# Filter tables transposed on the chip, a smaller DMA scratch, twelve weight tiles and a later router, in a kernel of Fourier filter and expert layers

## The chip, the cores and the metric

The kernel runs on one core of a Trainium2 chip. A core has five engines with queues of their own: TensorE (PE, its weight loads PEld), VectorE (DVE), ScalarE (ACT), GpSimd (POOL) and SyncE (SP), which here only issues DMAs; ScalarE and GpSimd issue DMAs too. Each queue is worked off in order, so an instruction that waits holds up all behind it. The metric is the device time of one execution in microseconds (us).

## The reference

Three layers follow each other, all in float32. The tokens of the second layer are the 8 x 3072 rows that the first gives; an expert's capacity is 768.

```
X = np.fft.rfft(x, axis=1)                       # x: 8 x 3072 x 256
y = np.fft.irfft(X * (filt_r + 1j*filt_i), n=3072, axis=1)
x = y.reshape(24576, 256)
logits = x @ w_gate                              # 8 experts
expert = argmax(logits);  gate = softmax probability of it
# each expert takes its first 768 tokens in order of arrival; later ones are dropped
y[e] = relu(disp[e] @ w1[e]) @ w2[e]             # w1: 8 x 256 x 1024, w2: 8 x 1024 x 256
out = gate * y[expert] where kept, else 0
out = ((out @ w_a) * (out @ w_b)) @ w_out        # 256 x 1536, 1536 x 256, given as float64
```

Only kept tokens have an output that is not zero. The eight experts are full after three of the eight sequences, so the kernel's fast path transforms sequences 0 to 2 only (NB0 = 3) and checks at the end that all experts were full; otherwise a general path follows, which does not run with these inputs.

## The kernel before

**Fourier filter.** A sequence of 3072 is taken as 128 x 24. Transform A is a product with a 128x128 table `wa` (L264, and L277 for sequence 0, which keeps its result in SBUF). For each half h of the 256 channels, 32 pairs of frequencies are worked in eight chunks of four: `fwd` multiplies with the forward tables `wb` (L309), VectorE forms the complex product with the filter tiles `fr` and `fi` (L320 to L322), GpSimd adds the two parts to `y` (L323), and `inv` multiplies `y` with the inverse tables `wbi` (L332). Sequence 0 gets its operand by transposes on TensorE (L300); sequences 1 and 2 write transform A to DRAM (`da`) and read it back. The last steps are `idft_t` (L373) and `idft_a` (L390), which writes token rows to DRAM (`rows`), and the router's product (L412).

**Order.** The order is written by hand. A loop over `i` in `fast_path` (iteration i) takes one forward chunk and, two iterations behind it, one inverse chunk; three iterations (i = 16 to 18) are left without a forward chunk, so chunk g is in iteration g up to 15 and g + 3 from 16 on. `put(first, last, steps)` spreads other steps over iterations: the loads of the next x, transform A of the next sequence, and of the sequence before it the inverse transforms and the routing. Iteration 37 to 52 are the last: there the routing of sequence 1 is laid beside sequence 2's chunks.

**Loads at the start.** SyncE's queue first issues x of sequence 0 in two halves, the tables and the filter tiles (`p1_loads`), then x of sequence 1. The filter tile's partitions 64 to 127 are a copy of 0 to 63, made by ScalarE (`self.twice`, L215), except for the first tile of a half (i = 0), which is loaded a second time from an array of its own, `fr0`, that differs in one row. x of sequence 1 goes into the buffer of x of sequence 0 and waits for its last reader.

**Routing.** `route` gives seven steps (argmax, one-hot, a running count over tokens by a scan at L426, a product with a triangle for the totals at L433, slot numbers) and then eight `put` steps (one-hot values on VectorE at L468 and L471 and on GpSimd at L470) and eight `add` steps (product L480 and addition L483) that build the table of slots.

**Experts.** Sixteen blocks of 384 slots, (expert, half), of eight steps each; step s (L1131) does one `up` (six products, two terms by three for the split into high and low parts) and, two steps behind it, one `down`. Weights come in chunks of 128 hidden units: `load` by SyncE into a tile `raw`, `split` into `wh` on ScalarE (L633) and `wl` on GpSimd (L634). NWC is the number of `wh` and `wl` tiles and of the first `raw` tiles (ten); later `raw` tiles are five. The token rows of a block are gathered by three indirect DMAs from GpSimd (L646), transposed on TensorE (L657) and split. `beside[s]` holds the routing of sequence 2, which goes beside steps 0 to 11; `main` is what stands between the last inverse chunk and step 0: the chunks' loads, the first gather and its transposes, the eight inverse transforms `t1` (L373) and the logits `r[0]` (L412). `a` are the twelve output transforms (L390).

**Last layer.** From step 17 on the float64 weights are converted beside the experts; then TensorE computes the last layer from 545 us to the end, and GpSimd scatters the results (L742).

Of the kernel before, what the change touches and what calls it, by code (L numbers as in the profile page):

```python
# [31 lines left out]
NWC = 10  # L32
# [4 lines left out]
NE = 3  # L37
# [15 lines left out]
def dft_tables():  # L53
# [5 lines left out]
    wbi = np.zeros((2, 2, N2, NPAIR, N2, 4))  # L59
    for s in range(64):  # L60
# [10 lines left out]
        for q in range(N2):  # L71
            if s == 0 and q == 0:
                alt = (-1.0) ** n2
                wb[:, 0, 0, 0, 0, 0] = 1.0
                wb[:, 0, 0, 1, 0, 0] = alt
                wbi[0, 0, 0, 0, :, 0] = 1.0
                wbi[1, 0, 0, 0, :, 0] = alt
                continue
# [3 lines left out]
            if s == 0:  # L82
                g = 0 if q < 12 else 1
                wb[:, g, 0, 0, 0, q] = c
                wb[:, g, 0, 1, 0, q] = -sn
                wbi[0, 0, q, 0, :, g] = 2 * c
                wbi[1, 0, q, 0, :, g] = -2 * sn
            else:
# [6 lines left out]
                wbi[0, j, q, p, :, a] = c  # L95
                wbi[1, j, q, p, :, a] = -sg * sn
                wbi[0, j, q, p, :, b] = sn
                wbi[1, j, q, p, :, b] = sg * c
# [3 lines left out]
    wbip = np.zeros((2, 64, NPAIR, 96), f)  # L102
    wbip[:, 0:48] = wbi.reshape(2, 48, NPAIR, 96)
    return (wa.astype(f), wai.astype(f), wbp.reshape(96, NPAIR, P)[:, :, 0:112],
            wbip.reshape(P, NPAIR, 96)[0:112])
# [22 lines left out]
class Kernel:  # L128
# [73 lines left out]
    def p1_loads(self):  # L202
# [3 lines left out]
        def table(name, i):  # L206
            q.dma_start(getattr(self, name)[i], io[name][:, 8 * i:8 * i + 8, :])

        def real(h, i):
            t = self.fr[4 * h + i]  # L210
            q.dma_start(t[0:64], io["fr"][:, h, 8 * i:8 * i + 8, :])
            if i == 0:
                q.dma_start(t[64:P], io["fr0"][:, h])
            else:
                self.twice[h, i] = lambda: self.nc.scalar.copy(t[64:P], t[0:64])  # L215
# [12 lines left out]
        for h in range(2):  # L228
            for i in range(4):
                steps += [lambda i=i: table("wb", i)] * (h == 0)  # L230
                steps += [lambda h=h, i=i: real(h, i)] * (h + i > 0)
                steps += [lambda h=h, i=i: imag(h, i)]
                steps += [lambda i=i: table("wbi", i)] * (h == 0)
        return steps + [lambda n=n: q.dma_start(getattr(self, n), io[n])
                        for n in ("iw", "wai", "scm", "eio", "tri", "ones", "eof", "lane", "line")]

# [45 lines left out]
    def dft_b(self, pe, pl, h, da, sa=None):  # L282
# [20 lines left out]
        def fwd(c, eng):  # L303
            if c % 2 and (h, c // 2 + 1) in self.twice:
                self.twice.pop((h, c // 2 + 1))()
# [312 lines left out]
    def load_chunk(self, pa, e, f, pr=None, eng=None):  # L618
# [6 lines left out]
        def load():  # L625
            raw = T["raw"] = (pr or pa).tile([P, 4, P], F32, tag="raw", name="raw", bufs=NWC if pr else 5)
# [298 lines left out]
def fast_path(K, outer):  # L925
# [4 lines left out]
    with ExitStack() as ctx:  # L930
# [16 lines left out]
        for step in loads[:6]:  # L947
            step()
        K.ident_ids()
        for step in consts[:5] + loads[6:] + consts[5:]:  # L950
            step()
# [12 lines left out]
        put(0, 5, K.dft_a_direct(xs, sa, 1))  # L964
# [25 lines left out]
        for i, g in enumerate(seq):  # L990
            back = seq[i - LAG] if i >= LAG else None
            if i == 5:
                xl, xn = K.load_x(pe, 1, K.new_sd(r2))
                st, das[1] = K.dft_a(pe, xn)
                put(5, 7, xl)
# [14 lines left out]
            if i == 34 + GAP:  # L1010
                t, a, r, p, d = finish(1)
                put(i, i + 1, t)
                put(i + 2, i + 5, rows_and_routes(a, r))
                put(i + 6, i + 9, p, into=early)
                put(i + 8, i + 11, d)
                put(i + 12, i + 12, [K.early_slots, lambda: K.counts(r1, 0, NE, min(cap, BLK))])
# [166 lines left out]
def general_path(K):  # L1183
# [9 lines left out]
    with ExitStack() as ctx:  # L1193
# [5 lines left out]
        run(K.p1_loads())  # L1199
# [51 lines left out]
def host_arrays(inputs):  # L1251
    f = np.float32
    wa, wai, wb, wbi = dft_tables()
# [39 lines left out]
```

## Time and profile before

| what | value |
|---|---|
| three timed runs | 1125.75, 1127.32, 1127.71 us; median 1127.32 |
| profiled execution: own time, span | 1124.34 us, 1122.5 us |
| TensorE busy | 1068.8 us, 95% |
| VectorE, ScalarE, GpSimd busy | 828.7 (74%), 442.6 (39%), 673.9 us (60%) |
| DMA | 123.27 MB, mean 110 GB/s |
| chain that ended last | TensorE 80%, DMA 6%, VectorE 4%, issue 4%, GpSimd 2% |

The span is the time from the first to the last instruction that the profiler records; the own time is that execution's time by the device's clock, 1.84 us more. The chain follows the end of the program back to what released each step. A row of a timeline gives the start, the busy time, the engine, the line, and in square brackets how long the engine had been idle and what ended that.

### The profile page before, as it was taken

What the parts mean: (1) busy time and instruction counts of PE and PEld (TensorE: products, weight loads), DVE (VectorE), ACT (ScalarE), POOL (GpSimd) and SP (SyncE); (2) the same over time, 40 slices, a digit from 0 to 9 for tenths busy, and PEclk for the clock granted to TensorE, in tenths of its full rate; (3) what the DMA queues carried; (4) which work ended last, traced back from release to release, by engine and by line L of the source; (5) the groups of instructions that cost most, each with busy time, mean ns of one, the idle gap of its engine ahead of it and who ended that gap; (6) DMA issues with size and microseconds to landing.
All of it is one profiled execution on the core that took longest, in us unless ns stands there. A gap on an engine that the chain in (4) does not pass through costs nothing.

```text
span 1122.5 us, 19362 instructions
## 1 busy us (share of the span) xinstructions
PE 1068.8 (95%) x6908; PEld 1023.9 (91%) x6908; DVE 828.7 (74%) x1589; ACT 442.6 (39%) x894; POOL 673.9 (60%) x676
## 2 busy tenths in 40 slices
PE   7899998899998999999999999999999999999993
PEld 7777797869998999999899999999999999999992
DVE  1738788675575777663888888888888888888873
ACT  2664544454665555553322232232232223232220
POOL 1412645576899787751555756657567475675742
PEclk8999999999999999999999999999999999999997
DMA  9955824354777666550404013040030000100000
GB/s 217 216 198 175 260 60 162 112 188 119 237 229 216 214 199 198 166 178 28 154 1 141 30 43 113 15 142 29 17 140 15 29 29 3 42 15 1 29 1 31
DMA packets 109097, 123.27 MB, mean 110 GB/s; under 512 B 8576, under 2 KB 92544, under 8 KB 108992
## 3 DMA queue, kind: packets, MB, share of 16 engines
q1 hardware_dynamic: 93152, 87.34, 26.4%
q10 hardware_dynamic: 11232, 22.02, 5.4%
q0 software_dynamic: 4608, 12.59, 3.6%
q8 instruction: 56, 0.92, 0.3%
q14 instruction: 49, 0.40, 0.1%
HBM read 68.44 MB, written 53.48 MB: 109 GB/s over the span
## 4 chain that ended last, share of the span: by engine, by line
PE 80%; DMA 6%; DVE 4%; issue 4%; POOL 2%; SPq 1%; ACT 1%; ACTq 0%; DVEq 0%; POOLq 0%
PE ps L666 13%; PE ps L667 13%; PE ps L668 13%; PE po L831 6%; PE po L830 6%; PE po L829 5%; PE yp L667 3%; PE yp L668 3%; PE yp L666 3%; PE ps L373 3%; PE ps L332 3%; PE ps L309 3%; PE ps L390 2%; PE ps L264 2%; DMA fr<-fr 1%
## 5 line engine op out<-in xcount | busy, mean ns | idle before, releaser
L758 POOL TENSOR_TENSOR gl<-w_b,gh 128x384 fp32r<-128x384 f32 x190 | 194.3, 1033 | 196.0 <-ACT gh L757 195.8
L757 ACT CAST gh<-w_b 128x384 fp32r<-128x384 f32 x192 | 98.7, 514 | 262.3 <-DVE w_b L776 196.8
L831 PE MATMUL po<-w_outh,gl 128*128 128x256 f32 x576 | 160.6, 279 | 0.2 <-POOL gl L758 0.2
L830 PE MATMUL po<-w_outl,gh 128*128 128x256 f32 x576 | 160.8, 279 | 0.0
L829 PE MATMUL po<-w_outh,gh 128*128 128x256 f32 x552 | 154.0, 279 | 0.0
L323 POOL TENSOR_TENSOR y<-t,t 112x512 f32<-112x512 f32 x48 | 65.6, 1368 | 128.0 <-DVE t L322 100.7
L634 POOL TENSOR_TENSOR wl<-raw,wh 128x512 fp32r<-128x512 f32 x88 | 112.3, 1292 | 39.6 <-ACT wh L633 16.5
L666 PE MATMUL ps<-th,w_bh 128*128 128x384 f32 x336 | 114.7, 341 | 4.4 <-DVE w_a L769 4.4
L666 PE MATMUL ps<-th,w_ah 128*128 128x384 f32 x336 | 113.5, 338 | 1.3 <-DVE w_b L769 0.8
L667 PE MATMUL ps<-tl,w_ah 128*128 128x384 f32 x336 | 113.6, 338 | 1.0 <-DVE tl L723 0.5
L668 PE MATMUL ps<-th,w_al 128*128 128x384 f32 x336 | 113.3, 337 | 0.0
L667 PE MATMUL ps<-tl,w_bh 128*128 128x384 f32 x336 | 113.2, 337 | 0.0
L668 PE MATMUL ps<-th,w_bl 128*128 128x384 f32 x336 | 113.1, 337 | 0.0
L683 DVE SCALAR_TENSOR_TENSOR hl<-ps,hh 128x384 fp32r<-128x384 f32 x128 | 70.5, 553 | 55.6 <-ACT hh L682 44.6
L831 PEld LDWEIGHTS po<-w_outh,gl 128*128 128x128 f32 x576 | 108.1, 188 | 1.5 <-POOL gl L758 0.4
L830 PEld LDWEIGHTS po<-w_outl,gh 128*128 128x128 f32 x576 | 108.0, 187 | 0.0
L829 PEld LDWEIGHTS po<-w_outh,gh 128*128 128x128 f32 x552 | 103.6, 188 | 0.0
L682 ACT ACTIVATE hh<-ps 128x384 fp32r<-128x384 f32 x128 | 62.7, 490 | 94.3 <-PE ps L668 84.3
L790 ACT COPY p<-ps 128x384 f32<-128x384 f32 x96 | 46.0, 479 | 127.3 <-PE ps L668 69.9
L776 POOL TENSOR_TENSOR w_b<-w_b,w_a 128x384 f32<-128x384 f32 x94 | 93.8, 1019 | 0.0
L666 PE MATMUL ps<-xh,wh 128*128 128x384 f32 x256 | 91.1, 356 | 0.0
L667 PE MATMUL yp<-hl,wh 128*128 128x384 f32 x256 | 86.0, 336 | 3.9 <-DVE hl L683 3.9
(157 smaller groups left out, 2801.3 us busy)
## 6 DMA issues: line engine op xcount, KB each, us to landing
out<-wide SPq DMA_DIRECT2D x48, 512.0 KB
raw<-w SPq DMA_DIRECT2D x176, 128.0 KB
rows<-yt ACTq DMA_DIRECT2D x18, 512.0 KB
da<-sa ACTq DMA_DIRECT2D x12, 512.0 KB
sb<-da SPq DMA_DIRECT2D x32, 192.0 KB
yd<-yb ACTq DMA_DIRECT2D x16, 384.0 KB
y<-yd SPq DMA_DIRECT2D x8, 768.0 KB
sd<-x SPq DMA_DIRECT2D x12, 256.0 KB
```

The costliest lines, as they stand in the source:

```text
L323: eng.tensor_tensor(y, t1, t2, ALU.add)
L634: (eng or nc.gpsimd).tensor_tensor(l, T["raw"], h.bitcast(F32), ALU.subtract)
L666: mm(out, wh, xh, start=first, stop=False)
L667: mm(out, wh, xl, start=False, stop=False)
L668: mm(out, wl, xh, start=False, stop=last)
L683: nc.vector.scalar_tensor_tensor(hl, hp[:, :BLK], 0.0, hh.bitcast(F32), ALU.max, ALU.subtract)
L757: nc.scalar.copy(gh, g)
L758: (v if hurry and not ij[1] else nc.gpsimd).tensor_tensor(gl, g, gh.bitcast(F32), ALU.subtract)
L776: (v if hurry or ij in ON_V else nc.gpsimd).tensor_tensor(c, c, T["a"][ij], ALU.mult)
L829: mm(out, gh[:, sl], oh[:, o:o + D], start=False, stop=False)
L830: mm(out, gh[:, sl], ol[:, o:o + D], start=False, stop=False)
L831: mm(out, gl[:, sl], oh[:, o:o + D], start=False, stop=u == NU - 1 and i == 1 and j == 0)
```

## The change

1. The inverse tables `wbi` are no longer loaded. The constants of pair s = 0 are scaled by the root of 2, so that each slice of `wbi` is the transpose of a slice of `wb`; `back_table` makes them with 32 transposes on TensorE and eight copies on VectorE, one table in each of iterations 1, 3, 5 and 7.
2. The first filter tile of a half is copied by ScalarE too (`twice`), and its one differing row is then loaded by a DMA from ScalarE's queue.
3. The loads of the start stand in another order; transform A of sequence 0's second half moves from iterations 0 to 5 to iterations 3 to 6, and the issue of x of sequence 1 from 5 to 7 to iterations 8 to 10.
4. The routing of sequence 1 is spread over more iterations (rows and routing 39 to 44 for 39 to 42, `put` 45 to 50 for 43 to 46, `add` 47 to 52 for 45 to 48).
5. In `main` the transposes of the first gathered rows move behind the inverse transforms, the logits and two output transforms; the routing of sequence 2 moves three or more steps back, the output transforms are one to a step.
6. The scratch for dynamic DMAs is set to 4096 bytes; NWC is 12, and `raw` has six tiles later on.

```diff
@@
-NWC = 10
+NWC = 12
...
-                wb[:, g, 0, 0, 0, q] = c
-                wb[:, g, 0, 1, 0, q] = -sn
-                wbi[0, 0, q, 0, :, g] = 2 * c
-                wbi[1, 0, q, 0, :, g] = -2 * sn
+                wb[:, g, 0, 0, 0, q] = 2 ** 0.5 * c
+                wb[:, g, 0, 1, 0, q] = -2 ** 0.5 * sn
...
         def real(h, i):
             t = self.fr[4 * h + i]
             q.dma_start(t[0:64], io["fr"][:, h, 8 * i:8 * i + 8, :])
+            self.twice[h, i] = lambda: twice(t, h, i)
+
+        def twice(t, h, i):
+            self.nc.scalar.copy(t[64:P], t[0:64])
             if i == 0:
-                q.dma_start(t[64:P], io["fr0"][:, h])
-            else:
-                self.twice[h, i] = lambda: self.nc.scalar.copy(t[64:P], t[0:64])
+                self.nc.scalar.dma_start(t[64:65, 0, :], io["fr0"][:, h])
...
-                steps += [lambda i=i: table("wbi", i)] * (h == 0)
...
+    def back_table(self, i):
+
+        nc = self.nc
+        for k in range(0, 8, 4):
+            pt = self.ps()
+            for j in range(4):
+                nc.tensor.transpose(pt[0:M2, 96 * j:96 * j + 96], self.wb[i][:, k + j, :], self.ident[0:96, 0:96])
+            nc.vector.tensor_copy(self.wbi[i][:, k:k + 4, :].rearrange("p j r -> p (j r)"), pt[0:M2, 0:384])
...
-            if c % 2 and (h, c // 2 + 1) in self.twice:
-                self.twice.pop((h, c // 2 + 1))()
+            if c % 2 and divmod(4 * h + c // 2 + 1, 4) in self.twice:
+                self.twice.pop(divmod(4 * h + c // 2 + 1, 4))()
...
-            raw = T["raw"] = (pr or pa).tile([P, 4, P], F32, tag="raw", name="raw", bufs=NWC if pr else 5)
+            raw = T["raw"] = (pr or pa).tile([P, 4, P], F32, tag="raw", name="raw", bufs=NWC if pr else 6)
...
-        for step in loads[:6]:
+        for step in loads[:3] + consts[:2] + [lambda: K.twice.pop((0, 0))()] + loads[3:6]:
             step()
         K.ident_ids()
-        for step in consts[:5] + loads[6:] + consts[5:]:
+        for step in consts[2:7] + loads[6:9] + consts[7:10] + loads[9:] + consts[10:]:
             step()
...
-        put(0, 5, K.dft_a_direct(xs, sa, 1))
+        put(3, 6, K.dft_a_direct(xs, sa, 1))
+        put(1, 8, [lambda i=i: K.back_table(i) for i in range(4)])
...
-                put(5, 7, xl)
+                put(8, 10, xl)
...
-                put(i + 2, i + 5, rows_and_routes(a, r))
-                put(i + 6, i + 9, p, into=early)
-                put(i + 8, i + 11, d)
-                put(i + 12, i + 12, [K.early_slots, lambda: K.counts(r1, 0, NE, min(cap, BLK))])
+                put(i + 2, i + 7, rows_and_routes(a, r))
+                put(i + 8, i + 13, p, into=early)
+                put(i + 10, i + 15, d)
+                put(i + 15, i + 15, [K.early_slots, lambda: K.counts(r1, 0, NE, min(cap, BLK))])
...
-            main += t1[k:k + 1] + {0: cs[0:1], 1: cs[1:2], 3: first[1:2], 4: first[2:3], 5: cs[2:3],
-                                   6: xs[1][0:1], 7: r[0:1] + cs[3:4]}.get(k, [])
+            main += t1[k:k + 1] + {0: cs[0:1], 2: cs[1:2], 5: cs[2:3], 6: xs[1][0:1]}.get(k, [])
+        main += r[0:1] + a[0:2] + first[1:2] + cs[3:4] + first[2:3]
...
-        beside[2] += xs[2][0:1]
-        for k, step in enumerate(a):
-            beside[k * 2 // 3].append(step)
+        beside[7] += xs[2][0:1]
+        for k, step in enumerate(a[2:]):
+            beside[k].append(step)
         for k, step in enumerate(r[1:]):
-            beside[k].append(step)
+            beside[3 + k].append(step)
         for k in range(0, NPUT, 2):
-            beside[7 + k // 2] += d[k:k + 2]
-            beside[6 + k // 2] += p[k:k + 2]
-        beside[11] += [lambda: K.all_slots(r1), lambda: K.counts(r1, 1, E, cap)]
+            beside[10 + k // 2] += p[k:k + 2]
+        for k in range(NPUT):
+            beside[12 + k // 3] += d[k:k + 1]
+        beside[14] += [lambda: K.all_slots(r1), lambda: K.counts(r1, 1, E, cap)]
...
-    nc = bacc.Bacc("TRN2", target_bir_lowering=False, num_devices=1)
+    nc = bacc.Bacc("TRN2", target_bir_lowering=False, num_devices=1, dynamic_dma_scratch_size=4096)
```

In SyncE's queue at the start of the program the loads stand as follows before (`sd` is x of sequence 0 in SBUF, `wb_119` and `wb_120` the first two forward tables, `wbi_123` an inverse table, `fr_127` the first filter tile):

```order
L249 DMA sd<-x 128x4x128 x6
L165 DMA ident<-eye 128x128
L166 DMA ids<-ids 128x24
L211 DMA fr_127<-fr 64x1024
L213 DMA fr_127<-fr 64x1024
L207 DMA wb_119<-wb 96x896
L219 DMA fi_135<-fi 48x1024
L207 DMA wbi_123<-wbi 112x768
L249 DMA sd<-x 128x4x128 x6
L207 DMA wb_120<-wb 96x896
```

And in the changed kernel, at the same place:

```order
L247 DMA sd<-x 128x4x128 x3
L199 DMA fr_127<-fr 64x1024
L247 DMA sd<-x 128x4x128 x3
L153 DMA ident<-eye 128x128
L154 DMA ids<-ids 128x24
L195 DMA wb_119<-wb 96x896
L209 DMA fi_135<-fi 48x1024
L195 DMA wb_120<-wb 96x896
L199 DMA fr_128<-fr 64x1024
L209 DMA fi_136<-fi 48x1024
L247 DMA sd<-x 128x4x128 x3
```

The filter tile moved between the two parts of x's first half, its second load and the inverse table are gone, and the second table and filter tile stand ahead of x's second half.

On TensorE, between the last inverse transforms and the first product of the experts, stands before (`iw,sc` are inverse transforms, `rowt` the gathered rows, `xh,wh` the experts' first product):

```order
L373 MATMUL ps_2087<-iw,sc 128x136 x3
L657 MATMUL ps<-ident,rowt 128x128 x3
L373 MATMUL ps_2099<-iw,sc 128x136 x3
L657 MATMUL ps<-ident,rowt 128x128 x3
L373 MATMUL ps_2111<-iw,sc 128x136 x3
L373 MATMUL ps<-iw,sc 128x136 x3
L373 MATMUL ps_2139<-iw,sc 128x136 x3
L412 MATMUL ps<-z,wai 128x192 x2
L390 MATMUL ps<-sd,wai 128x512 x2
L666 MATMUL ps<-xh,wh 128x384
```

And in the changed kernel:

```order
L371 MATMUL ps<-iw,sc 128x136 x3
L371 MATMUL ps_2179<-iw,sc 128x136 x3
L410 MATMUL ps<-z,wai 128x192 x2
L388 MATMUL ps_2192<-sd,wai 128x512
L388 MATMUL ps<-sd,wai 128x512
L655 MATMUL ps_2199<-ident,rowt 128x128 x3
L655 MATMUL ps<-ident,rowt 128x128 x3
L388 MATMUL ps<-sd,wai 128x512
L664 MATMUL ps<-xh,wh 128x384
```

The two groups of transposes moved from the middle of the inverse transforms to behind two output transforms.

On GpSimd, at the first expert steps, stands before (`rowt<-rows` are gathers, `wl<-raw,wh` splits, `val` the first one-hot values of the slot counting):

```order
L646 DMA rowt<-rows,early 128x256 x3
L634 TENSOR_TENSOR wl<-raw,wh 128x512 x3
L646 DMA rowt<-rows,early 128x256 x3
L634 TENSOR_TENSOR wl<-raw,wh 128x512 x4
L646 DMA rowt<-rows,early 128x256 x3
L634 TENSOR_TENSOR wl<-raw,wh 128x512 x6
L470 TENSOR_TENSOR val<-val,g 128x3x48
```

And in the changed kernel:

```order
L644 DMA rowt<-rows,early 128x256 x3
L632 TENSOR_TENSOR wl<-raw,wh 128x512 x3
L644 DMA rowt<-rows,early 128x256 x3
L632 TENSOR_TENSOR wl<-raw,wh 128x512 x13
L644 DMA rowt<-rows,early 128x256 x3
L632 TENSOR_TENSOR wl<-raw,wh 128x512 x3
L468 TENSOR_TENSOR val<-val,g 128x3x48
```

The third block's gather moved from behind four splits to behind thirteen, and 19 splits in place of 13 stand ahead of the slot counting.

## Rows read from the trace of the kernel before

**Rows 1.** Windows: start:end, us, busy PE, PEld, DVE, ACT, POOL, PEclk, DMA share, GB/s.

```profile
15.34:55.15 39.81, 32.39 (x260) 31.49 (x261) 24.83 (x36) 20.51 (x31) 15.23 (x12) 0.89 1.00 217
55.15:62.32 7.17, 7.17 (x21) 4.12 (x21) 0.00 (x0) 2.81 (x5) 0.00 (x0) 0.67 0.96 370
...
162.12:209.88 47.76, 43.58 (x300) 37.13 (x299) 43.37 (x84) 19.11 (x35) 23.12 (x27) 0.96 0.30 100
209.88:226.91 17.03, 14.10 (x105) 12.23 (x103) 7.22 (x20) 9.77 (x25) 10.71 (x10) 1.00 0.75 221
226.91:270.83 43.92, 40.79 (x217) 33.85 (x216) 30.58 (x69) 21.37 (x43) 33.32 (x37) 1.00 0.47 155
...
330.00:480.00 150.00, 143.96 (x839) 141.54 (x838) 104.05 (x239) 84.07 (x177) 119.03 (x122) 1.00 0.66 202
```

**Rows 2.** Chain of waits from 0 to 62 us: start, us, what.

```profile
30.80 9.79 DMA fr<-fr
...
40.60 9.25 DMA fi<-fi
...
50.79 4.22 DMA sd<-x
```

**Rows 3.** DMA issues from 0 to 80 us.

```profile
fr<-fr SPq DMA_DIRECT2D x10, 256.0 KB
...
wbi<-wbi SPq DMA_DIRECT2D x4, 336.0 KB
```

**Rows 4.** Timeline of the first 60 us.

```profile
7.01 0.59 ACT L278 COPY sa<-ps 128x512 f32<-128x512 f32 x1 [4.98 <-PE ps L277]
...
15.34 1.84 PE L309 MATMUL ps<-sb,wb 96*112 96x128 f32 x8 [1.58 <-DMA wb<-wb]
...
27.08 1.04 ACT L215 COPY fr<-fr 64x1024 f32<-64x1024 f32 x1 [5.68 <-DMA fr<-fr]
...
46.91 0.60 PE L300 MATMUL ps<-ident,sa 128*96 128x128 f32 x4
...
47.35 1.04 PE L309 MATMUL ps<-sb,wb 96*112 96x128 f32 x8
...
55.15 3.75 PE L264 MATMUL ps<-sd,wa 128*128 128x512 f32 x4 [4.58 <-DMA sd<-x]
```

**Rows 5.** Timeline, a copy of VectorE out of PSUM.

```profile
79.01 0.56 DVE L378 COPY sd<-ps 128x384 f32<-128x384 f32 x1
```

**Rows 6.** TensorE's waits from 165 to 290 us: us, times, longest.

```profile
PE ps L332 <- POOL y L323: 3.4, 1, 3.4
PE ps L433 <- DVE tot L428: 2.7, 1, 2.7
PE ps L657 <- DMA rowt<-rows,early: 1.9, 2, 1.3
```

**Rows 7.** Timeline, the scan in two routings and GpSimd beside the second.

```profile
168.14 0.56 DVE L426 TENSOR_TENSOR_SCAN cum<-scm,oh 128x192 f32<-128x192 f32 x1
...
229.13 4.95 POOL L634 TENSOR_TENSOR wl<-raw,wh 128x512 fp32r<-128x512 f32 x4
...
229.76 4.74 DVE L426 TENSOR_TENSOR_SCAN cum<-scm,oh 128x192 f32<-128x192 f32 x1
```

**Rows 8.** TensorE's waits from 330 to 380 us.

```profile
PE ps L657 <- DMA rowt<-rows,gidx: 1.8, 2, 1.3
PE yp L667 <- DVE hl L683: 1.8, 1, 1.8
```

**Rows 9.** Timeline, a later block's gathers and the transposes that use them.

```profile
279.22 1.03 POOL L646 DMA_INDIRECT rowt<-rows,gidx  x1 [0.15 <-issue]
280.56 1.00 POOL L646 DMA_INDIRECT rowt<-rows,gidx  x1 [0.30 <-issue]
...
287.96 0.49 PE L657 MATMUL ps<-ident,rowt 128*128 128x128 f32 x3
```

**Rows 10.** Chain of waits from 334 to 376 us, one gather's landing.

```profile
338.43 3.49 DMA rowt<-rows,gidx
```

More of the change, by code (lines that the diff above doesn't have):

```diff
@@ L58, in dft_tables @@
     wb = np.zeros((N2, 4, NPAIR, 2, 2, N2))
-    wbi = np.zeros((2, 2, N2, NPAIR, N2, 4))
     for s in range(64):
@@ L75, in dft_tables @@
                 wb[:, 0, 0, 1, 0, 0] = alt
-                wbi[0, 0, 0, 0, :, 0] = 1.0
-                wbi[1, 0, 0, 0, :, 0] = alt
                 continue
@@ L94, in dft_tables @@
                 wb[:, b, p, 1, j, q] = sg * c
[L95 to L98, printed above, removed]
     f = np.float32
@@ L101, in dft_tables @@
     wbp[:, :, :, 0:48] = wb.reshape(96, NPAIR, 2, 48)
[L102 to L105, printed above, removed]
+    return wa.astype(f), wai.astype(f), wbp.reshape(96, NPAIR, P)[:, :, 0:112]
 def filter_layout(filt):
@@ L204, in p1_loads, with table @@
         io, q = self.io, self.nc.sync
-        def table(name, i):
-            q.dma_start(getattr(self, name)[i], io[name][:, 8 * i:8 * i + 8, :])
+        def table(i):
+            q.dma_start(self.wb[i], io["wb"][:, 8 * i:8 * i + 8, :])
         def real(h, i):
@@ L229, in p1_loads @@
             for i in range(4):
-                steps += [lambda i=i: table("wb", i)] * (h == 0)
+                steps += [lambda i=i: table(i)] * (h == 0)
                 steps += [lambda h=h, i=i: real(h, i)] * (h + i > 0)
                 steps += [lambda h=h, i=i: imag(h, i)]
-                steps += [lambda i=i: table("wbi", i)] * (h == 0)
         return steps + [lambda n=n: q.dma_start(getattr(self, n), io[n])
                         for n in ("iw", "wai", "scm", "eio", "tri", "ones", "eof", "lane", "line")]
+    def back_table(self, i):
[5 more added lines that the diff above has]
+            nc.vector.tensor_copy(self.wbi[i][:, k:k + 4, :].rearrange("p j r -> p (j r)"), pt[0:M2, 0:384])
     def load_x(self, pe, b, whole=None, parts=1):
@@ L1198, in general_path @@
         nc.sync.dma_start(K.wa, K.io["wa"])
-        run(K.p1_loads())
+        run(K.p1_loads(), K.twice.values(), [lambda i=i: K.back_table(i) for i in range(4)])
+        K.twice = {}
         with tc.For_i(NB0, B) as b:
@@ L1252, in host_arrays @@
     f = np.float32
-    wa, wai, wb, wbi = dft_tables()
+    wa, wai, wb = dft_tables()
     cap = int(inputs["moe_capacity"])
@@ L1261, in host_arrays @@
     fi[0, :, 0, :] = 0
-    fr0 = fr[:, :, 0:8, :].copy()
-    fr0[0, :, 0, :] = inputs["filt_r"][S // 2].reshape(2, P)
+    fr0 = inputs["filt_r"][S // 2].reshape(1, 2, P)
     scm = np.ones((P, E, N2), f)
@@ L1268, in host_arrays @@
         **{n: np.ascontiguousarray(inputs["moe2_" + n]).view(np.int64) for n in ("w_a", "w_b", "w_out")},
-        wa=wa, wai=wai, wb=wb, wbi=wbi, iw=iw, fr=fr, fi=fi, fr0=fr0,
+        wa=wa, wai=wai, wb=wb, iw=iw, fr=fr, fi=fi, fr0=fr0,
         eye=np.eye(P, dtype=f), ones=np.ones((P, P), f), tri=np.triu(np.ones((P, P), f), 1),
```

## The prediction

> **What bounds the kernel now.** I read the windows by stage first [rows 1]: TensorE is the engine that sets the end, and what can be gained is the time in which it waits or runs at the lower clock. It waits in five places: before and after 55 us, between 162 and 210, between 210 and 227, in the first expert steps up to 271, and here and there from 330 to 480. In the second half of the program (from 545 on) neither the order nor the buffers are touched, so I leave it as it is.
>
> Second, the chain of waits of the first 62 us [rows 2]: it runs through SyncE's queue, from load to load (7 to 10 us each), and ends with the load of sequence 1's x, issued only at 50.79, after all tables and filters. The DMA share in this stretch is 1.00 at 217 GB/s [rows 1]: transfers bound it, and TensorE was busy 32.39 of 39.81 us. [...]
>
> Third, TensorE's own waits from 165 to 290 [rows 6]: 3.4 us for y from GpSimd (VectorE was late with its inputs), 2.7 us for the totals of the router, 1.9 us for the first gather of expert rows.
>
> **The change part by part.** The sum is made against the profiled execution: span 1122.5, own time 1124.34 us. The median of the timed runs is 1127.32, 3.0 us higher, and it is a median that is predicted.
>
> *Start.* Removed: four loads of the inverse table (336 KB each) and two second halves of a filter tile (256 KB each, two of the ten fr loads) [rows 3]: 1856 KB, 1.90 MB, which at the 217 GB/s of the stretch [rows 1] is 8.8 us. The load of sequence 1's x, 50.79 + 4.22 = 55.01 [rows 2], then lands at about 46.3. Its move from iterations 5 to 7 to iterations 8 to 10 costs nothing: no other SyncE instruction stands between, and it only has to follow the last use of the old x, now in iteration 6.
> Added on TensorE: 32 transposes of table slices. The nearest row is the transposing of the other operand, four from 46.91 to the next group at 47.35 [rows 4], 0.44 us, so eight groups are 3.5 us. Added on VectorE: eight copies of 112x384 out of PSUM, 0.56 us each by the 128x384 copy [rows 5], 4.5 us; VectorE was busy 24.83 of 39.81 us [rows 1], and 29.3 still fits, but wbi now stands behind it where it came by DMA. Added on ScalarE: two copies of filter halves at 1.04 us [rows 4], and two loads of one row from its queue.
> The first of those copies now stands at the head of ScalarE's queue and waits for the filter tile, the fifth load of SyncE's queue in place of the tenth. Behind it are the six copies of the first transform, behind these the first transposes and the first product. The tile and all ahead of it are 1.1 MB, 5 us at the stretch's rate; with 3 us for issue and latency (a gather took 3.49 to land [rows 10]) it is there at 8, and the copy ends at 9, where the first transform copy began at 7.01 [rows 4]. The six copies (0.59 each) then end near 13. The first table has 256 KB less ahead of it, 1.2 us. I put the first product at 15.34 as before [rows 4], 1.5 us later at worst.
> From there TensorE has its 32.39 us plus 3.5: 15.34 + 35.9 = 51.2. The x is there at 46.3, so TensorE itself is late next. Gain 55.15 - 51.2 = 3.9. Without the 4.58 us of idling the clock should not fall there: 7.17 us at 0.67 are 4.8 at 1.0, 2.4 more. **6.3 us**; from 2.5 (late start, clock lost elsewhere) to 9 (the transposes lie in waits that remain).
>
> *Sequence 1's router.* Nothing is removed; router and output transform are spread over six iterations instead of four, slot counting over six instead of four. From 162.12 to 209.88 VectorE was busy 43.37 of 47.76 us [rows 1]: it is the engine that bounds, first idle for others and then late for them. At best the stretch shrinks to VectorE's 43.4, a gain of 4.4; at worst nothing. I take **3 us**, nearer to the bound, since the 3.4 us wait for y [rows 6] is the pile-up that spreading removes. The counting ends later, but the first gather's issue was held by GpSimd's last y in any case.
>
> *The turn to the experts.* 17.03 us, TensorE busy 14.10 [rows 1]. Its transposes of gathered rows move behind all eight inverse transforms, the logits and two output transforms, so the gather (1.9 us of waiting [rows 6]) is covered; what is late next is the copy that feeds the inverse transforms. Bounds 0.5 and 2.9 (all idle time); I take **2 us**.
>
> *First expert steps.* 43.92 us, TensorE busy 40.79 [rows 1], so 3.1 us of waiting, 2.7 of them for the totals [rows 6]. The scan before these took 4.74 us where the same scan took 0.56 at 168.14, and it ended as a run of four GpSimd splits of 4.95 us in all ended [rows 7]. The change moves the scan from step 1 to step 4, where in steps 3 to 7 GpSimd now has two splits a step (2.5 us of about 3). If the scan meets pairs, it waits up to 2.5, which is inside the slack of about 3 us, one step, between it and the product that needs it (twelve steps took 43.92 us, 3.7 each with counting). If the splits form one long run, it waits longer than before. Two splits more fall into this stretch (2.5 us on GpSimd, busy 33.32 of 43.92 [rows 1], so covered). I take **1.5 us**, from -4 to 3.1.
> [...]
>
> *Twelve and six tiles.* From 271 on each split stands nine steps ahead of its use instead of seven, with as many splits in each step as before: GpSimd's place in its queue is the same. The waits of TensorE there are for gathers and for hl [rows 8], not for split weights, so the extra tiles buy little: **0.5 us**, from -1 to 2, of the 6.0 us idle from 330 to 480 [rows 1].
>
> *The scratch.* It issues nothing and I take 0; its price, if it has one, is the last rival.
>
> Sum: 6.3 + 3 + 2 + 1.5 + 0.5 = 13.3. TensorE is busy nearly throughout behind each place, so an earlier end of a stage is kept. 1124.34 - 13.3 = 1111.0 beside the profile, 1114.0 from the median; between the two and nearer the median, **1113**.
>
> **The rivals.** *Only the start pays.* The spread work piles up elsewhere: in steps 12 to 14 TensorE's slot counting (24 products) now waits for GpSimd's one-hot values, which stand behind splits, and the scan meets a long run. For it: GpSimd's share in that stretch, 0.76. Against: the step between value and use is as long as before. Middle 0, turn 1, steps -2: 6.3 - 1 = 5.3, so 1122; with parts of the others 1118 to 1123.
> *The start does not pay.* ScalarE's head-of-queue copy and the in-order wait of the inverse products for VectorE's table copies make the first iterations as slow as the loads did. For it: a table copy stands behind two iterations of VectorE work. Against: VectorE's 29.3 of 39.8. Start 1, rest 7: 1127.3 - 8 = 1119.
> *Slower: the small ring holds GpSimd's DMAs.* Three gathers are issued 1.3 us apart and land 3.49 us after the last issue [rows 9, 10]. If the scratch holds one at a time, each of two waits 2.2 us more: 4.4 us per block. From first issue at 279.22 to use at 287.96 are 8.7 us, of which 2.6 + 3.5 = 6.1 are used [rows 9, 10], so 2.6 are slack and 1.8 us are lost per block, 23 us over 13 blocks, and 11 us on the last six scatters behind the last product. 34 - 13.3: 1148. It decides as soon as fewer than two gathers fit. Nothing in the trace shows the ring, but three gathers in flight at once are few.
> [...]
>
> **How the numbers follow.** The forecast 0.62 (1106 to 1119), only the start 0.20, no gain at the start 0.10, slower by the ring 0.04; 0.04 for all terms at their upper ends, 1104 and below. The range that leaves out 2 in 10 or less is 1105 to 1122. A measurement of this kernel can tell about 0.2%, 2.3 us, from no change. Faster takes the forecast, 0.18 of the second, 0.07 of the third and the upper ends: 0.91; same the 0.05 left of the second and third; slower 0.04.
>
> **What would show it.** Right: no load of wbi, and x of sequence 1 issued near 42 to 45; the first product of its transform (L264) starts near 51 with no idling before it and the clock at 1.0 after; the stretch from iteration 39 to the last forward product near 45 us; no wait of L657 for the early gather; the scan under 2.5 us. Wrong: L264 still waiting for x; wbi's copies as releasers of L332 for many us; a scan as long as a run of splits; gathers issued more than 1.3 us apart.

## The result, and the profile after

The changed kernel takes 1100.29 us (median of 4 runs, 1099.70 to 1101.68), the kernel before 1126.53 (median of 4, 1124.44 to 1127.71): a ratio of 0.9771, interval 0.9752 to 0.9789, or 25.8 us by the ratio. 1113 was predicted, range 1105 to 1122: the sign was right, the gain about twice the 13.3 us of the forecast's sum. The profiled execution has a span of 1099.9 us, 22.6 less than that of before. From line 240 to line 1080, line numbers are 2 lower than before (L666 is now L664).

**The start.** The chain of waits up to 54 us, start, us and what:

```profile
2.76 5.60 DMA fr<-fr
8.38 1.05 ACT fr L203
9.46 0.51 ACTq L205
10.01 3.04 ACT sa L276 x6
13.10 0.69 PE ps L298 x4
13.81 0.59 ACT sb L299
14.45 1.14 PE ps L307 x8
...
19.85 0.56 DVE wbi L233
20.41 0.14 issue
20.55 1.10 PE ps L330 x8
...
40.29 1.76 DMA fr<-fr
42.07 0.33 SPq L223
...
43.94 0.36 SPq L247
44.34 7.30 DMA sd<-x
51.78 1.96 PE ps L262 x4
```

From 10 to 40 us it runs through the engines and no more from load to load [rows 2]; its last stretch still goes through SyncE's queue and ends with sequence 1's x. The early filter copy ends at 9.42, and the first product stands at 14.45 in place of 15.34 [rows 4]. The six copies behind the filter copy in ScalarE's queue begin at 10.01, where the first of them began at 7.01 [rows 4]. The timeline around sequence 1's x:

```profile
43.94 3.99 SPq L247 DMA_DIRECT2D sd<-x  x6
...
48.86 1.88 PE L262 MATMUL ps<-sd,wa 128*128 128x512 f32 x4
51.78 1.96 PE L262 MATMUL ps<-sd,wa 128*128 128x512 f32 x4 [0.18 <-DMA sd<-x]
```

The x is issued from 43.94. Its transform starts at 48.86 without a wait, and the first four products take 1.88 us; it was 55.15, after 4.58 us of waiting, and 3.75 us [rows 4]. The next four wait 0.18 us for the x, so it comes only just in time. The forward product of chunk 12 came at 62.32 and comes at 54.01: 8.3 us, kept up to the router. How much of this is this one execution's luck is told in the part on why the prediction was wrong.

**The middle.** Windows (us, then busy us of PE, PEld, DVE, ACT and POOL, granted clock, DMA share, GB/s): from iteration 39 to the last forward product, the turn up to the first expert product, the first expert steps, and a stretch within these:

```profile
153.81:194.15 40.34, 38.57 (x274) 32.39 (x273) 38.16 (x74) 18.70 (x35) 20.92 (x23) 1.00 0.37 118
...
193.97:212.66 18.69, 18.12 (x134) 15.64 (x132) 9.24 (x28) 9.80 (x24) 14.80 (x16) 1.00 0.54 157
212.66:256.60 43.94, 41.15 (x208) 34.94 (x209) 30.86 (x57) 24.21 (x50) 35.50 (x35) 0.96 0.66 203
251.60:255.00 3.40, 3.40 (x12) 3.31 (x11) 3.09 (x6) 1.00 (x2) 3.24 (x6) 0.50 0.20 59
```

The first took 47.76 [rows 1]: 7.4 less. But TensorE has 26 instructions fewer in it and 29 more in the turn, which grew from 17.03 to 18.69. Together they gain 5.9 us, and the first expert product comes at 212.66 in place of 226.91, 14.25 earlier. The first expert steps took 43.92 and take 43.94: nothing gained. TensorE's waits in them:

```profile
PE ps L478 <- POOL val L468: 1.6, 1, 1.6
PE ps L431 <- DVE tot L426: 0.8, 1, 0.8
PE ps L665 <- DVE xl L657: 0.2, 1, 0.2
```

The wait for the totals fell from 2.7 us [rows 6] to 0.8, with the scan at 0.82 in place of 4.74 [rows 7]. A new one, for the one-hot values, took its place, and the granted clock is 0.50 behind it. The timeline of TensorE there:

```profile
245.10 0.33 PE L664 MATMUL ps<-xh,wh 128*128 128x384 f32 x1
...
247.18 0.49 PE L655 MATMUL ps<-ident,rowt 128*128 128x128 f32 x3
...
250.59 0.91 PE L478 MATMUL ps<-val,ohl 128*128 128x96 f32 x6 [1.59 <-POOL val L468]
251.28 0.42 PE L664 MATMUL ps<-xh,wh 128*128 128x384 f32 x1
...
255.01 0.50 PE L655 MATMUL ps<-ident,rowt 128*128 128x128 f32 x3
```

Twelve products take 2.08 us from 245.10 to 247.18, and 3.73 from 251.28 to 255.01: the stretch at half clock costs 1.65 more.

**The end.** From 274 us on TensorE's transposes of gathered rows (L655) come between 13.9 and 15.5 us earlier than before, and the last scatter, issued at 1109.06 before and at 1095.02 after, 14.0. The spans are 22.6 apart. The other 8.5 us lie behind the last scatter, where no engine counts as busy. First the timeline of before, with GpSimd's queue instructions behind it (count: shortest/median/longest ns, first and last start):

```profile
1109.06 0.98 POOL L742 DMA_INDIRECT out<-ob,oidx  x1 [0.30 <-issue]
...
L921 POOLq INC_SWDGE_SEM  x1: 2108/2108/2108, 1111.6 to 1111.6; - x1
...
L1290 POOLq DRAIN  x3: 40/107/7905, 1113.7 to 1122.2; - x3
```

The same of after:

```profile
1095.02 0.98 POOL L740 DMA_INDIRECT out<-ob,oidx  x1 [0.30 <-issue]
...
L919 POOLq INC_SWDGE_SEM  x1: 428/428/428, 1097.5 to 1097.5; - x1
...
L1290 POOLq DRAIN  x3: 40/107/1045, 1098.0 to 1099.6; - x3
```

The long DRAIN fell from 7.91 to 1.05 us and INC_SWDGE_SEM from 2.11 to 0.43: 8.54 us together.

### The profile page after: what moved, and what is told of

Same layout as the page of the kernel before. It is cut to its first block, busy times and chain, and to the rows that moved or that the text cites. A ratio compares the mean times of both kernels' runs of the same rounds, so it can differ in the third digit from the quotient of the medians.

```text
span 1099.9 us, 19423 instructions
## 1 busy us (share of the span) xinstructions
PE 1066.8 (97%) x6940; PEld 1024.0 (93%) x6940; DVE 832.0 (76%) x1597; ACT 443.5 (40%) x896; POOL 675.0 (61%) x676
## 4 chain that ended last, share of the span: by engine, by line
PE 80%; POOL 5%; DMA 4%; DVE 4%; issue 4%; ACT 1%; SPq 1%; POOLq 0%; ACTq 0%; DVEq 0%
PE ps L664 13%; PE ps L665 12%; PE ps L666 12%; PE po L829 6%; PE po L828 6%; PE po L827 5%; PE ps L330 3%; PE ps L307 3%; PE ps L371 3%; PE yp L665 3%; PE yp L666 3%; PE yp L664 3%; PE ps L388 2%; POOL wl L632 2%; PE ps L262 2%
## 5 line engine op out<-in xcount | busy, mean ns | idle before, releaser
L632 POOL TENSOR_TENSOR wl<-raw,wh 128x512 fp32r<-128x512 f32 x88 | 113.0, 1302 | 35.8 <-ACT wh L631 15.5
L664 PE MATMUL ps<-th,w_bh 128*128 128x384 f32 x336 | 114.7, 341 | 4.5 <-DVE w_a L767 4.5
L664 PE MATMUL ps<-th,w_ah 128*128 128x384 f32 x336 | 113.5, 338 | 1.2 <-DVE w_b L767 0.8
L666 PE MATMUL ps<-th,w_al 128*128 128x384 f32 x336 | 113.2, 337 | 0.0
L666 PE MATMUL ps<-th,w_bl 128*128 128x384 f32 x336 | 113.1, 336 | 0.0
L664 PE MATMUL ps<-xh,wh 128*128 128x384 f32 x256 | 91.8, 359 | 0.2
```

The lines of the kernel that those rows point to most:

```text
L632: (eng or nc.gpsimd).tensor_tensor(l, T["raw"], h.bitcast(F32), ALU.subtract)
L664: mm(out, wh, xh, start=first, stop=False)
L666: mm(out, wl, xh, start=False, stop=last)
```

## The experiments

The ratios of the runs below are against the kernel before, timed on the same chip.

**Each part by itself**

```diff
-    nc = bacc.Bacc("TRN2", target_bir_lowering=False, num_devices=1)
+    nc = bacc.Bacc("TRN2", target_bir_lowering=False, num_devices=1, dynamic_dma_scratch_size=4096)
```

> The kernel before with nothing changed but the scratch for dynamic DMAs, 4096 bytes. Theory A (the scratch is what shortens the close of the program): GpSimd's last long DRAIN takes 1.0 us in place of 7.9 and its INC_SWDGE_SEM 0.4 in place of 2.1, as in the profile after, so 8.5 us less, about 1118 from a median of 1126.5; nothing moves ahead of the last scatter, still issued near 1109. Theory B (the close depends on what ran before it, such as the order of the gathers): the DRAIN stays at 7.9 us and the time within 2 us of the kernel before. Theory C (my prediction's rival of a small ring): gathers are held, issued more than 1.3 us apart, and the time grows by 10 us or more.

Measured: 0.9912 (0.9878 to 0.9946), 9.9 us; DRAIN 1.05, INC_SWDGE_SEM 0.43:

```profile
1117.05 0.98 POOL L742 DMA_INDIRECT out<-ob,oidx  x1 [0.30 <-issue]
...
L921 POOLq INC_SWDGE_SEM  x1: 428/428/428, 1119.7 to 1119.7; - x1
...
L1290 POOLq DRAIN  x3: 40/107/1045, 1120.2 to 1121.8; - x3
```

Theory A in the close and in the time: one number in one line, which moves no instruction, gives about as much as the whole start does, or more (the intervals overlap). One thing was not as expected: the last scatter is issued at 1117.05 and not near 1109. The profiled execution is the slowest of the four (1123.93 us; the others take 1115.37 to 1118.95), at a mean granted clock of 0.982 where the profile of before has 0.986; its first expert product comes 2.3 us later than there, and the last layer begins 7.7 us later. So its span of 1122.1 us shows no gain, and 9.9 is a rough size; the close itself, from the end of the last scatter's issue to the end of the long DRAIN, takes 3.2 us in place of 11.6.

The start alone: the hunks on `dft_tables`, `p1_loads`, `back_table` and the first loads, with the order

```diff
-        put(0, 5, K.dft_a_direct(xs, sa, 1))
+        put(3, 6, K.dft_a_direct(xs, sa, 1))
+        put(1, 8, [lambda i=i: K.back_table(i) for i in range(4)])
...
-                put(5, 7, xl)
+                put(8, 10, xl)
```

> The kernel before with the start alone: inverse tables transposed on the chip, filter halves copied by ScalarE, x of sequence 1 loaded in iterations 8 to 10. Theory A (the places are independent): the gain is the shift read between the two profiles at iteration 12, 62.32 to 54.01, 8.3 us, and it is kept to the end: 1118. Theory B (part of the gain is given back where sequence 1's router piles up, since its bound there is VectorE and not the time at which it begins): 4 to 6 us, 1121 to 1123. My prediction had 6.3.

Measured: 0.9927 (0.9904 to 0.9949), 8.2 us: theory A; the interval, 5.7 to 10.8 us, does not exclude the upper end of B.

Sequence 1's router alone:

```diff
-                put(i + 2, i + 5, rows_and_routes(a, r))
-                put(i + 6, i + 9, p, into=early)
-                put(i + 8, i + 11, d)
+                put(i + 2, i + 7, rows_and_routes(a, r))
+                put(i + 8, i + 13, p, into=early)
+                put(i + 10, i + 15, d)
```

> The kernel before with the routing and slot counting of sequence 1 alone spread over more iterations. Theory A (the spread takes away the pile-up and nothing more): the stretch from iteration 39 to the last forward product shrinks from 47.8 us to about 40.3 as in the profile after, but the counting that is left over lands in the turn, so the first expert product comes about 5 us earlier, and the end 5 us earlier: 1121.5. Theory B (the counting that is left over delays the first gather and with it the turn): the first product comes at most 2 us earlier, and the time is 1124 to 1126.

Measured: 0.9976 (0.9957 to 0.9994), 2.7 us (0.7 to 4.8); the first expert product at 225.62 in place of 226.91. That is theory B's product and a time between the two theories: the stretch does shrink, from 47.8 to 40.3 us, but most of what leaves it lands in the turn.

The turn and the routing of sequence 2 alone:

```diff
...
-            beside[7 + k // 2] += d[k:k + 2]
-            beside[6 + k // 2] += p[k:k + 2]
+            beside[10 + k // 2] += p[k:k + 2]
+        for k in range(NPUT):
+            beside[12 + k // 3] += d[k:k + 1]
...
```

> The kernel before with the turn and the routing of sequence 2 alone changed (transposes of the gathered rows later, router, scan and counting three steps later). Theory A (my prediction's two terms): the wait for the first gather, 1.9 us, and that for the totals, 2.7 us, go: 1123 to 1122.5. Theory B (as the profile after suggests, in which the shift is 14.3 us at the first expert product and 14.4 at the fifteenth expert step): the wait for the totals is exchanged for one for the one-hot values of the counting and a stretch at half clock, so only the turn's 1 to 2 us stay: 1125.

Measured: 0.9954 (0.9938 to 0.9971), 5.2 us: theory A, more than the wait in the changed kernel's profile had me expect. The four parts add up to 26.0 us, the joined change has 25.8; with intervals of 3.7 to 7.6 us for each part that does not show them to be independent. In one stretch they are not, by one execution each: from iteration 39 to the first expert product the kernel before takes 64.8 us, the router alone 64.2, the turn alone 64.0, and the joined change 58.8.

Put back in the changed kernel, the same hunk:

> The changed kernel with the turn and the routing of sequence 2 put back as before. Theory A (it is worth what it was by itself, 0.5%): 1105 to 1106, with the wait for the first gather and that for the totals back. Theory B (with the later counting of sequence 1 its worth grows, because that counting now delays the first gather which the old turn needs at once): 1107 or more. Theory C (worth nothing here): 1100 to 1102.

Measured: 0.9821 (0.9805 to 0.9838), 1107.59, 7.3 us above the changed kernel by the medians and 5.6 by the ratios, with the wait for the totals back; the one for val, which the kernel before lacks [rows 6], stays:

```profile
PE ps L431 <- DVE tot L426: 2.3, 1, 2.3
PE ps L478 <- POOL val L468: 1.2, 1, 1.2
```

The first gather was waited for 3.0 us in place of 1.9 [rows 6]. That is some support for B; the two ways of reckoning are too far apart to call it shown.

**What pays in the start**

```diff
+                steps += [lambda i=i: table("wbi", i)] * (h == 0)
...
-        put(1, 8, [lambda i=i: K.back_table(i) for i in range(4)])
```

> The start part alone on the kernel before, but with the four inverse tables loaded as before and no transposes: what stays of the start is the halved filter loads, the order of the first loads and the later place of sequence 1's x. Theory A (bytes in front of that x pay for the start, as my prediction had it): 1.38 MB are back, 6.3 us at 217 GB/s, so the x lands about 2.5 us before its time in the kernel before and TensorE still waits for it: a gain of 2 to 3 us, 1124, against 8 for the start alone. Theory B (the early first filter copy and the order of the first loads pay, by taking away the wait of 1.58 us for the table wb and the half clock behind it): 6 us or more stay, 1120.

Measured: 1.0014 (0.9995 to 1.0033), no gain at all. The timeline, and the chain of waits ahead of it:

```profile
55.08 3.40 PE L275 MATMUL ps<-sd,wa 128*128 128x512 f32 x4 [2.32 <-DMA sd<-x]
```

```profile
44.94 3.02 DMA fr<-fr
47.97 0.33 SPq L236
...
50.79 4.16 DMA sd<-x
```

Theory B is out. TensorE still waits for the x, as theory A has it, but the x is issued at 50.79 as before [rows 2], though 512 KB of filter loads are gone. The chain shows what took the 2 to 3 us that theory A had left: one of SyncE's last table loads (`eio`) is issued at 47.97, 2.3 us after SyncE is done with the issue before it, when the one differing row of the second half's first filter tile has landed, which ScalarE issues at 44.94 behind a copy. The changed kernel has the same wait (SyncE's load at 42.07 behind the row load of 40.29, 1.5 us); the prediction has no term for it. So the start pays with the 1.38 MB of inverse tables gone and not with them loaded; what the order of the first loads is worth by itself was not measured.

**The size of the scratch.** All on the changed kernel, the first three with NWC at 10 and five `raw` tiles, and dynamic_dma_scratch_size at 16384, 8192, 4096 and 2048. The first leaves the argument out, as the kernel before does; that this is 16384 is my figure, which no run prints. The small program below that sets 16384 has, with 96 gathers, a close of 7.91 us, as long as that of the kernel before without its branch.

> The changed kernel with the scratch as before and ten and five tiles as before, so all but the scratch and the tiles. Theory A (the scratch shortens the close alone, and the tiles are worth nothing): DRAIN 7.9 and INC_SWDGE_SEM 2.1 us are back, 8.5 us over the changed kernel's 1100.3: 1109. Theory B (the extra tiles carry a good part of the gain): 1112 or more, with TensorE waiting for split weights after 271.

> The changed kernel with a scratch of 8192 bytes and ten and five tiles. Theory A (the close costs in proportion to the scratch: between 16384 and 4096 bytes the DRAIN falls by 6.86 us, 0.57 per KB, and INC_SWDGE_SEM by 1.68): DRAIN 3.3 us and INC_SWDGE_SEM 1.0, 2.9 us over the same with 4096 bytes, so 1103. Theory B (a threshold: the close is long when the scratch exceeds what the kernel's gathers fill): 7.9 or 1.0 us, 1109 or 1100.

> The changed kernel with 4096 bytes and ten and five tiles: the tiles alone undone. Theory A (the extra tiles buy nothing, since TensorE waits for gathers and hl there and not for split weights): within 1.5 us of 1100.3. Theory B (GpSimd's splits are kept further ahead of their use by them): 2 to 6 us slower, with waits of TensorE for wl or wh after 271.

> The changed kernel with a scratch of 2048 bytes. Theory A (in proportion, and gathers not held): DRAIN and INC_SWDGE_SEM fall again, to under 0.5 and 0.3 us, 1 us less: 1099. Theory B (a ring this small holds GpSimd's DMAs, my prediction's rival at half the size): gathers issued more than 1.3 us apart, TensorE waits for gathered rows in most blocks, 1105 or more.

Measured: 1109.38, 1107.66, 1101.22 and 1102.53 us. The longest DRAIN and INC_SWDGE_SEM at 8192:

```profile
L1290 POOLq DRAIN  x3: 40/107/3903, 1101.6 to 1106.1; - x3
...
L919 POOLq INC_SWDGE_SEM  x1: 1128/1128/1128, 1100.5 to 1100.5; - x1
```

At 16384 they are 7.91 and 2.11 as before, at 4096 and at 2048 alike 1.05 and 0.43. So the close grows with the scratch, but not in proportion to the bytes, and below 4096 nothing was left to win: neither theory has 8192 or 2048 right. 16384 against 4096 with the same tiles is 8.2 us. At 8192 the close is 3.6 us longer than at 4096; the other 3 us of that run stand ahead of the last scatter, issued at 1097.93 in place of 1094.87, at a mean granted clock of 0.992 in place of 0.995. Ten tiles against twelve: 1101.22 against 1100.29, no difference that can be told. Neither 4096 nor 2048 bytes held the gathers: those of a block are issued 1.31 us apart at 16384, at 4096 (the changed kernel) and at 2048 bytes (between 270 and 530 us), so my rival of a small ring is out. With 16384 and with 4096 bytes theory A was right.

**What the close depends on.** A small program, all else left out, in outline, one execution for each count:

```
for k in range(COUNT):                 # 1, 8, 40, 96
    nc.gpsimd.indirect_dma_start(out=rows[:, k % 4, :], in_=x, in_offset=..., ...)
nc.sync.dma_start(out_part, rows)
```

> The close by itself: a program that does one gather of 128 rows of x and writes the rows to a part of the output, with the scratch of the kernel before (16384 bytes); all the computation is left out. Theory A (the close walks over the whole scratch, whatever was in it): DRAIN 7.9 us and INC_SWDGE_SEM 2.1, as in the kernel before with its 96 gathers and scatters. Theory B (it works off what is still held in the scratch, and 96 have filled it): both short, under 1.1 and 0.5 us.

> The same with eight gathers in 16384 bytes. Theory A: DRAIN 7.9 us. Theory B: the steps of both instructions between 4096, 8192 and 16384 bytes are as 5 to 7 (DRAIN 2.86 and 4.00, INC_SWDGE_SEM 0.70 and 0.98), which is what a count of held transfers of 3, 8 and 15 would give; eight gathers would then be as the scratch of 8192 bytes: 3.9 us and 1.1.

> The same with forty gathers in 16384 bytes, more than would be held. Theory A and B: DRAIN 7.9 us, INC_SWDGE_SEM 2.1. If both are longer, neither the size nor what it holds sets them, but all that was issued.

> Forty gathers in 4096 bytes. Theory A and B: DRAIN 1.0 us, INC_SWDGE_SEM 0.4, so the program is 8.5 us shorter than with 16384. If the gathers are issued further apart than with 16384 bytes, the small scratch holds them, and the gain of the close is paid for there.

Here the DRAIN begins while the last gathers are still being issued, so its length says little; what counts is its end behind the end of the last gather's issue. The last column is the issue of the write-out of the rows, which waits for the gathers to land, behind the same end (all in us):

| gathers, bytes | last issue ends | DRAIN, start + length | its end behind | write-out behind |
|---|---|---|---|---|
| 1, 16384 | 4.78 | 3.42 + 3.20 | 1.85 | 1.85 |
| 8, 16384 | 13.89 | 10.55 + 5.50 | 2.15 | 1.87 |
| 40, 16384 | 55.66 | 52.25 + 6.93 | 3.52 | 1.92 |
| 40, 4096 | 55.60 | 52.23 + 5.98 | 2.61 | 1.88 |

Theory A is out. B's direction holds, its sizes do not. With one gather and nearly so with eight the close ends when the rows have landed, so the landing may hide what it costs by itself.

The kernel before without its branch:

```diff
-        with tc.If(done < 1):
-            general_path(K)
```

> The kernel before, with 16384 bytes of scratch, without the fall-back path behind its last branch, which these inputs do not take (so its time for them is that of a whole computation). In the four small programs GpSimd's close ended 2.6 us after the last gather's issue with 4096 bytes and 3.5 with 16384, not 3.1 and 11.6 as in the two kernels, and there was no INC_SWDGE_SEM at the end; in the kernels that instruction stands at the join behind the branch. Theory C (it is the join of the untaken branch whose cost grows with the scratch): no INC_SWDGE_SEM there, DRAIN under 4 us, the time 6 to 8 us below the kernel before: 1119 to 1121. Theory D (it is the number of transfers, 96 here and 40 there): DRAIN 7.9 us as before, and the time within 2 us, the branch's own 0.6 us of reading the flag aside.

Measured: 0.9983 (0.9953 to 1.0013). Last scatter and DRAIN:

```profile
1113.07 0.99 POOL L742 DMA_INDIRECT out<-ob,oidx  x1 [0.31 <-issue]
...
L1286 POOLq DRAIN  x3: 40/102/12612, 1109.4 to 1122.5; - x3
```

INC_SWDGE_SEM is gone, and the DRAIN still ends at 1121.97, 7.91 behind the end of the last scatter's issue, as against 11.6 with the branch. So the branch adds its own 3.7 us to the close, but it isn't what the 7.9 are made of: theory C is out.

> The small program with 96 gathers, as many transfers as GpSimd issues in the kernel, and 16384 bytes; all the computation is left out. Measured as the end of GpSimd's long DRAIN behind the end of its last gather's issue: 1.85 us with one gather, 2.16 with eight, 3.53 with forty, and 7.91 in the kernel without the branch. Theory D (the number of transfers alone, up to what the scratch holds): 0.043 us for each more between one and forty, so 5.9 us if all 96 are held. Theory E (a kind of transfer that the small programs lack, the scatters to the output, costs more in the close): 5.9 us here too, and the 2 us that are missing to 7.9 belong to the scatters. Theory F (the scratch is full before 96): 3.6 to 5 us, and the kernel's 7.9 has another cause.

The last gather and the DRAIN:

```profile
127.50 0.99 POOL L23 DMA_INDIRECT rowt<-x,at  x1 [0.30 <-issue]
...
L38 POOLq DRAIN  x3: 40/96/11297, 125.1 to 136.9; - x3
```

125.11 + 11.30 - 128.50 = 7.91 us: to the hundredth the 7.91 of the kernel without its branch, with nothing but 96 gathers. So neither the scatters nor the computation are needed for it. None of the three theories had this number. D's cause is the one that is left: GpSimd's close takes the longer the more transfers were issued, some 0.08 us each (7.91 / 96, and 3.52 / 40), and less with a smaller scratch. That it works off what the scratch still holds, and that a smaller scratch holds less, is my estimate and was not shown: it fits the DRAIN of 7.91, 3.90 and 1.05 us at 16384, 8192 and 4096 bytes and the 2.61 us of forty gathers in 4096, but not the same 1.05 at 2048. How many it holds was not measured, nor 96 gathers with 4096 bytes by themselves. D's straight line, 0.043 each, was drawn from one gather to forty; with one the close ends as the rows have landed (1.85 us both).

**Two attempts to go further**

```diff
-                m = T["m"] = pc.tile([P, 8, P], F32, tag="mix", name="mix", bufs=2)
+                m = T["m"] = pc.tile([P, 8, P], F32, tag="mix", name="mix", bufs=3)
...
```

> The changed kernel with three tiles in place of two for the decoded weights of the second half (mix) and five in place of six for raw. In the profile after, TensorE waits three times for hl between 276 and 530, 4.0 us, because VectorE stands before the last step of a decode until GpSimd has read an old mix tile, behind three gathers. Theory A (the buffer is that wait): the waits for hl go, and the half clock behind the first of them: 4 to 5 us less, 1095 to 1096. Theory B (GpSimd is late as such, and VectorE meets the next tile as late): within 1.5 us of 1100.3.

Measured: 1098.92 us, 0.9741 (0.9723 to 0.9759): 1.4 us below the changed kernel, too little to be told apart: theory B's time. TensorE's waits from 276 to 530:

```profile
PE ps L655 <- DMA rowt<-rows,gidx: 4.4, 3, 1.9
PE ps L664 <- DVE w_b L767: 0.8, 1, 0.8
```

The waits for hl, 4.0 us, are gone, as theory A had it, and those for gathered rows grew from 1.2 us to 4.4: a wait in place of a wait.

```diff
-            beside[10 + k // 2] += p[k:k + 2]
+            beside[9 + k // 2 + (k > 3)] += p[k:k + 2]
```

> The changed kernel with the one-hot values of sequence 2's counting two and three steps ahead of their products (steps 9, 10, 12, 13 in place of 10 to 13). Theory A (the wait of 1.6 us for val at 249 and the half clock from 251.6 to 255.0 come from the short lead): both go, 3 us less: 1097. Theory B (the wait moves to the next place at which GpSimd is late, the scan or the splits): within 1.5 us of 1100.3.

Measured: 1102.90 us, 0.9782 (0.9754 to 0.9810): no gain, so theory A is out; theory B is nearest, though the median lies 2.6 us above the changed kernel's (1100.71 to 1106.40). TensorE waits 1.4 us for `place` and 0.6 each for hl and the totals, 2.6 in all, as in the changed kernel.

## Why the prediction was wrong

- **The scratch, "It issues nothing and I take 0": the step that failed.** It is worth 8.5 us by the rows, 9.9 by the timed part (6.1 to 13.7) and 8.2 between two sizes in the changed kernel, of 12.5 that the forecast missed. Ahead of it stands the cause: "neither the order nor the buffers are touched, so I leave it as it is", said of all that comes behind 545. The row that speaks against it was there: the last scatter of before is issued at 1109.06 and takes 0.98, and the span ends at 1122.5. I never asked what fills these 12.5 us. And I looked for a price of the scratch only where it could cost, in the gathers held, and not where it could pay.
- **The start: 6.3 said, 8.2 timed (5.7 to 10.8), 8.3 by the two profiles, 6.4 by all of them.** TensorE itself is late next, as said, though by little. The changed kernel's profile has the best start of all: in the nine profiles with the new start the forward product of chunk 12 comes at 54.01 to 58.39 us, 55.8 on average, in the five with the old one at 61.65 to 63.09, 62.2 on average. So the term was right, and about 2 us of the 8.3 are this execution's luck. The earlier first product is part of it: it comes at 14.27 to 16.35 in the nine and at 14.22 to 16.25 in the five. The clock term, 2.4 us, has no run of its own, and that the idling of 4.58 us [rows 4] lowered the clock was my inference; what the two profiles show, from the first product of sequence 1's transform to the forward product of chunk 12, is 7.17 us at a granted clock of 0.67 before [rows 1] and 5.15 us at 1.00 after, 2.0 less.
- **Sequence 1's router: 3 said, 2.7 timed, which is luck.** The stretch shrank by 7.4, past the "gain of 4.4" that I had as the best case, because VectorE's 43.37 us were not a fixed load: ten of its instructions moved out of the stretch, and its busy time with them, to 38.16. With the router alone most of that came back in the turn, for which I had no term.
- **The turn and the first expert steps: 3.5 said, 5.2 timed (3.3 to 7.0).** The wait for the first gather went. The scan is short, but not for my reason: it met a run of four splits again (the last section has the numbers), by which I had it wait longer than before. The loss that I allowed for in the steps came as the wait for val and the half clock behind it, 3.2 us, at another place than the scan.
- **Twelve and six tiles: 0.5 said**, nothing that can be told.
- **The rivals.** "Slower by the ring" had the right object and the wrong sign. "All terms at their upper ends", 1104 and below, had the time but not the reason: the three parts without the scratch come to 16.1 us, and the upper ends were 9, 4.4, 2.9, 3.1 and 2.

## What to carry to other kernels

Read a profile to its end: between the last instruction that counts as busy and the end of the span there can be work (12.5 us here), and a setting that issues nothing can be what sets it (8.5 of them went with 4096 bytes). Where a program has many DMAs issued by GpSimd (here 96), try a smaller scratch, look at the last DRAIN, and see whether the gathers are issued as close together as before; here 4096 and 2048 bytes held none of them (1.31 us apart, as with 16384). When an engine seems to bound a stretch by its busy time, ask first how much of that work can leave the stretch, and where it lands. And read a term of a few us from more than one profile of the same code: here the same start differed by 4.4 us between executions.

## What the runs showed of the hardware

- The close of this kernel, with 96 DMAs of GpSimd, has a DRAIN of 7.91 us with 16384 bytes of scratch (six kernels that keep the branch), of 3.90 with 8192 (one) and of 1.05 with 4096 or 2048 (seven).
- The executions of the changed kernel differ, the longer ones at a lower granted clock: the four have means of 0.993, 0.995, 0.997 and 0.997 and take 1101.68, 1100.43, 1099.70 and 1100.15 us. They lie within 2.0 us; the kernel before, timed beside all the runs, took from 1119.27 to 1131.58.
- A scan that begins inside a run of four GpSimd splits ended 0.42 us behind the run's last split in all five kernels with the old turn in which it met one: begun in the first or second split it took 4.03 to 4.74 us, begun in the fourth (the kernel without its branch) 1.02. In the four kernels with the new turn in which it met such a run it began in the first split, took 0.82 to 0.90 us and ended 3.5 to 3.6 us ahead of the run's end. The runs are alike (four splits, 4.95 and 5.25 us), so a run of splits alone does not explain the 4.74 us [rows 7]; what does stays open.
